# One transfer per weight load, wider loads of x, and a different deal of sums, transposes, taps and scalings in a fused convolution and GELU kernel

## The chip, the cores and the metric

The kernel runs on one core of a Trainium2 chip. A core has five instruction queues that run side by side and meet only through semaphores: TensorE (PE; its weight loads are shown as PEld), VectorE (DVE), ScalarE (ACT), GpSimd (POOL) and SyncE (SP), which here issues only transfers. Each queue is worked through in order. The transfers themselves run on 16 DMA engines that all queues share. Sums and copies run over 128 partitions at once. Results of TensorE go to PSUM, all other operands lie in SBUF. The metric is device time of one execution in microseconds.

## What is computed

The reference, cut to what matters. x is 8 sequences of 4096 tokens with 192 values; 8 heads of 24 values share a 7-tap causal filter each, softmaxed; then a feed-forward block with 2048 hidden values.

```python
w = np.exp(weight - weight.max(-1, keepdims=True))
w = w / (w.sum(-1, keepdims=True) + 1e-09)              # (8 heads, 7 taps)
x_pad = np.concatenate([zeros((B, 6, D)), x], axis=1)
x = einsum('hk,bskhg->bshg', w, windows_of_7(x_pad))    # causal convolution
h = x.reshape(32768, 192) @ w_in                        # w_in: 192 x 2048
g = h * (1.0 / (1.0 + np.exp(-1.702 * h)))              # quick GELU
out = g @ w_out                                         # w_out: 2048 x 192
```

w_in and w_out arrive as float64 and are turned into float32 on the chip, word by word.

## The kernel before

**Tiling.** The work is cut into 32 steps (`N_BIG`). A step takes 512 tokens (`TOK`) of two sequences, kept as two halves o = 0, 1 of 256 tokens on partitions 0-63 and 64-127. Per step the 2048 hidden values are 16 *units* (`NF`) of 128. Every step has two products.

**Hidden product** (`hidden`, L209 matmuls). A unit is three passes of six matmuls into a PSUM slot (a pair of banks, four slots in turn): x and w are split into a high and a low part in a rounded format (fp32r), so that xh with wh (`upper_high`), xl with a low part of w (`upper_low`), then a scaling of the slot by `UP` on ScalarE or VectorE (`scale`, L232), then xd with a third form of w (`lower`), then two GELUs from PSUM into g on ScalarE (`gelu`, L236). On TensorE the order is, for unit i: high part of i, last pass of i-2, low part of i. So a scaling has to be done between the low pass of its unit and the last pass two units on. The string for each unit in `SCALES` deals the two halves' scalings: "a" to ScalarE, "v" to VectorE. wh and half of the low parts stay in SBUF. The other three forms for two units come round through a `ring` of 7 slots, reloaded from `w_dram` by SP as soon as TensorE is done with a slot (`load_ring`, `later`), 24 loads a step.

**Second product** (`second`, L542 matmuls). It follows a list written out by hand (`PLAN`): fast-multiplication sums of blocks of g and of w_out ("spots", each 128 x 1024) replace some products. Ten of the sums of blocks are due while the hidden product still runs (`EARLY_G`); the loop at the end (`extra`) hands them out by unit. Numbers 0 to 4 and 6 to 9 are sums of two spots (L605), number 5 is an accumulating transfer issued from GpSimd (L610): spot 8 takes up spot 0. Sum 3 makes spot 0, sums 6 to 9 need spot 8 after the transfer. Near the end of the second product the next step's first passes are issued ("next").

**x.** Step b+2's x is loaded during step b's hidden product into the last block row of g (`load_x`, `xin_of`), 32 x 32 blocks are transposed on VectorE into `xt` (`transpose_x`, L143, three a step), and taps of the convolution run on ScalarE in the second product (`tap`, L498): each product of a tap goes to a home of its own, and homes are added into `own` by accumulating transfers and by GpSimd (`add_taps`, L515). The last three taps run in the next hidden product, and a tap that reuses a home has to wait for the sum that read it.

**First step** (`first_step`). Weights come in as float64 words, are joined and rounded (`split`, `join`, `rounded`), w_in by pieces of 256 columns: half on partitions 0-63 and half on 64-127, so that after rounding four SP transfers copy them to both halves; then `split_w_in` makes the three forms and stores the streamed ones to `w_dram`. The step's own hidden product waits for each piece. Its second product is plain (`second_plain`), while w_out's forms are made (`add_forms`) by copies on ScalarE and accumulating transfers from GpSimd.

Of the kernel before, what the change touches and what calls it, by code (L numbers as in the profile page):

```python
# [16 lines left out]
def kernel(  # L17
# [27 lines left out]
    XW = NC * Q  # L45
# [73 lines left out]
    x_p = x_v.rearrange("h p s (c v e) -> h p v s c e", c=NC, e=Q)  # L119
# [5 lines left out]
    def load_x(big, part=None):  # L125

        p, c = divmod(big, CHUNKS)
        xin = xin_of(big)
        if c == 0 and not part:
            (nc.gpsimd if big else vec).memset(xin[0:R, :, 0, :], 0.0)  # L130
        for i in range(8) if part is None else (part,):
            n, o, v = i // 4, i // 2 % 2, i % 2
            j = 1 if c == 0 and o == 0 else 0
            t = c * TOK + o * T + (j - 1) * Q
            q0 = o * R + v * Q
            for k in range(NC):
                nc.sync.dma_start(
                    out=xin[q0 : q0 + Q, n, j:NJ, k * Q : (k + 1) * Q],
                    in_=x_p[n, p, v, t : t + (NJ - j) * Q, k, :].rearrange("(j i) e -> i j e", i=Q),
                )  # L140

    def transpose_x(big, c):
        vec.transpose(  # L143
            xt[:, c, :, :].rearrange("p n (j t) -> p (n j) t", t=Q),
            xin_of(big).rearrange("p n j d -> p (n j) d")[:, :, c * Q : (c + 1) * Q],
        )
# [38 lines left out]
    w_dram = dram.tile([STREAM, R, NC * P], F32)  # L185
# [43 lines left out]

    def scale(slot, engines):  # L230
        for o in range(2):
            (act.mul if engines[o] == "a" else vec.tensor_scalar_mul)(slot[o], slot[o], UP)  # L232
# [13 lines left out]
    def hidden(big, tiles, scales, extra, begun=True):  # L246

        for i in range(NF):
            if i or not begun:
                upper_high(tiles[i % 4], i)  # L250
            if i > 1:
                end_unit(big, tiles, i - 2)
            if i or not begun:
                upper_low(tiles[i % 4], i, big)
# [52 lines left out]
    PART = NC * P  # L307
    PIECE = CW * D
    raw = [flat_g(2)[:, 2 * PART * i : 2 * PART * (i + 1)] for i in range(5)]
    raw += [osbs[:, 2 * PART * i : 2 * PART * (i + 1)] for i in range(2)]  # L310
    raw += [flat_own[:, 2 * T : 2 * T + 2 * PART]]
    raw_out = [flat_room[:, 2 * PIECE * i : 2 * PIECE * (i + 1)] for i in range(3)] + [osbs[:, 0 : 2 * PIECE]]
    assert 10 * PART <= 4 * BLK and 2 * PART <= 4 * T and NX <= 4 * BLK and 6 * PIECE <= 5 * BLK
    words_in = [flat_form[:, 2 * PART * i : 2 * PART * (i + 1)] for i in range(2)]
    both_in = [flat_form[:, 2 * PART * i : 2 * PART * (i + 1)] for i in range(2, 4)]
    words_out = [flat_form[:, 8 * PART + 2 * PIECE * i : 8 * PART + 2 * PIECE * (i + 1)] for i in range(2)]
    assert 8 * PART + 4 * PIECE <= FORMS * NG * HD
# [17 lines left out]
    w_in_v = moe_w_in.bitcast(U32).rearrange("(k q) (j h f) -> j h q k f", q=R, j=N_W, h=2)  # L335
# [43 lines left out]
    def in_part(j):  # L379
        return raw[j], words_in[j % 2]  # L380

    def out_piece(i):
        return raw_out[i], words_out[i % 2]
# [32 lines left out]
    def round_w_in(j):  # L416
# [3 lines left out]
        w = m.bitcast(F32)  # L420
        rounded(piece, [(lambda a: a, w)])
# [5 lines left out]
    def split_w_in(j):  # L427
        both = both_in[j % 2]
        act.mul(wh[:, 2 * j : 2 * j + 2].rearrange("p r k f -> p (r k f)"), both, DOWN)  # L429
        nc.gpsimd.tensor_sub(both, both, wide(wh[:, 2 * j : 2 * j + 2].rearrange("p r k f -> p (r k f)")))  # L430
        lows = [t.rearrange("p k f -> p (k f)") for t in (wl[:, j], in_ring(place("l", 2 * j + 1)))]
        for h in range(2):
            act.mul(lows[h], both[:, h * PART : (h + 1) * PART], C)  # L433
        for h in range(2):
            r = 2 * j + h
            to = in_ring(place("d", r)).rearrange("p k f -> p (k f)")
            nc.gpsimd.tensor_sub(to, wide(lows[h]), wide(wh[:, r].rearrange("p k f -> p (k f)")))
        for q in range(3 * j, 3 * j + 3):
            nc.sync.dma_start(out=w_dram[q], in_=wide(in_ring(q))[0:R].rearrange("p k f -> p (k f)"))
# [104 lines left out]
    def second_plain(bx, bs, by, at):  # L544

        mains, sides = (bs[0], bx[0], by[0]), (bx[1], bs[1], by[1])
        rows = [(r, i) for r in (0, 2, 1, 3) for i in range(NG)]
# [56 lines left out]
    def add_up(v, dst, a, op, b):  # L604
        (vec.tensor_add if op == "+" else vec.tensor_sub)(v(dst), v(a), v(b))  # L605

    def sum_g(dst, a, op, b=None):
# [3 lines left out]
        else:  # L611
            add_up(spot, dst, a, op, b)
# [86 lines left out]
    def first_src(c):  # L699
        src = own_of(0) if c == 0 else pairs[1][c - 1].rearrange("p (n t) -> p n t", n=2)  # L700
        return src, 2 * c, 2 * c + 2

    def first_step(tiles):
# [13 lines left out]
        for c in (1, 0, 2):  # L717
            split_high(*first_src(c))
            split_low(*first_src(c))
            split_both(*first_src(c))  # L720
        split_w_in(0)
        load_x(1)
        for i in range(3):
            load_w_out(i)

        def extra(i):
            if i % 2 == 0 and i // 2 + 1 < N_W:
                j = i // 2 + 1
                round_w_in(j)
                if j + 1 < N_W:  # L730
                    split(in_part(j + 1))
                split_w_in(j)
            if i in (9, 10, 11):
                transpose_x(1, i - 9)
            if i == 13:
                split(out_piece(0))
                load_w_out(3)
            if i == 15:
                split(out_piece(1))
                round_w_out(0)  # L740

        hidden(0, tiles, ["av", "vv"] * (NF // 2), extra, begun=False)
        end_unit(0, tiles, NF - 1)
        pf, pa, pb, pc = tiles[3], tiles[1], tiles[0], tiles[2]

        round_w_out(1)
        split(out_piece(2))
        split(out_piece(3))
        round_w_out(2)
        round_w_out(3)  # L750
        load_x(2)
# [3 lines left out]
        def at(i):  # L755
            if i == 0:
# [8 lines left out]
                for c in range(NC):  # L765
                    transpose_x(2, c)
            if i == 2:
# [17 lines left out]
        for c in range(NC):  # L785
            conv(c, 0, times=act.mul)
            for k in range(1, K):
                conv(c, k)
# [69 lines left out]
```

## Time and profile before

| | |
|---|---|
| Median of 3 runs | 2664.82 us (2663.09 to 2668.2) |
| Profiled execution | 2664.49 us, its span 2662.8 us |
| TensorE busy | 2345.8 us, 88% |
| VectorE busy | 1799.4 us, 68% |
| ScalarE busy | 1601.5 us, 60% |
| GpSimd busy | 754.4 us, 28% |
| DMA from GpSimd's queue / SP's queue | 34.3% / 31.7% of 16 engines' span |
| Mean granted TensorE clock | 0.965 |

How to read it: a row of a group has line, engine, operation, tiles written and read, shape, count, then busy time, mean nanoseconds of one, and how long the engine idled before them and for whom. A row of the order of time has start, duration and, in brackets, the idle time before it. A row of the table by stretch has the stretch, then the busy time of TensorE, its weight loads, VectorE, ScalarE and GpSimd with counts, the granted clock, the share of the DMA engines, and GB/s. A row of waits has who waited for whom, the total, how often, and the longest. A row of transfers has count, size and the median time from issue to landing. Matmuls are shown with modelled ends that overlap their followers.

### The profile page before, as it was taken

How to read it: one execution, taken by the hardware profiler on the slowest of the kernel's cores; microseconds unless marked ns; L12 is line 12 of the kernel's file. 1: busy time of each engine (PE TensorE's matmuls, PEld its weight loads, DVE VectorE, ACT ScalarE, POOL GpSimd, SP SyncE). 2: the span in 40 equal slices, each digit the busy share in tenths (PEclk: the TensorE clock that was granted, in tenths of full speed). 3: DMA queues.
4: the chain of work that ended last, by engine and by line, in shares of the span. 5: the costliest groups of instructions: out<-in, count | busy, mean ns of one | idle time of the engine just before them, and what ended most of it. 6: DMA issues, size and time to landing. Idle time of an engine off the chain costs nothing. (4 is left out here: it accounts for less than half of the span.)

```text
span 2662.8 us, 72405 instructions
## 1 busy us (share of the span) xinstructions
PE 2345.8 (88%) x28994; PEld 1561.1 (59%) x28994; DVE 1799.4 (68%) x2536; ACT 1601.5 (60%) x3142; POOL 754.4 (28%) x742
## 2 busy tenths in 40 slices
PE   4576999888999988899988899988999988889898
PEld 2434666556666555566656566656666656566566
DVE  3357667766667766667766667766667766666776
ACT  2444666665666665666665666665666666666654
POOL 1320333132233222233222233222233222233310
PEclk6798999999999999999999999999999999999999
DMA  5264777766777766677766677766667776677754
GB/s 130 58 119 107 151 145 154 155 148 140 148 144 154 158 146 141 147 144 153 153 145 142 147 144 153 154 150 138 146 143 154 155 153 143 144 146 150 159 122 104
DMA packets 525935, 378.64 MB, mean 142 GB/s; under 512 B 365472, under 2 KB 472096, under 8 KB 525600
## 3 DMA queue, kind: packets, MB, share of 16 engines
q0 software_dynamic: 63216, 162.49, 34.3%
q1 hardware_dynamic: 460736, 211.12, 31.7%
q8 instruction: 231, 3.78, 0.6%
q14 instruction: 104, 0.85, 0.1%
q10 hardware_dynamic: 1648, 0.39, 0.1%
HBM read 180.68 MB, written 27.53 MB: 78 GB/s over the span
## 5 line engine op out<-in xcount | busy, mean ns | idle before, releaser
L542 PE MATMUL slot<-g,w_form 128*32 128x256 f32 x8928 | 906.3, 380 | 0.0
L236 ACT ACTIVATE g<-slot 128x512 f32<-128x512 f32 x1024 | 551.0, 594 | 394.6 <-PE slot L209 386.6
L232 DVE TENSOR_SCALAR slot<-slot 128x512 f32<-128x512 f32 x644 | 435.1, 694 | 438.1 <-PE slot L209 404.9
L209 PE MATMUL slot<-xd,ring 64*128 64x512 f32 x3072 | 573.1, 411 | 129.2 <-DVE slot L232 104.6
L209 PE MATMUL slot<-xh,wh 64*128 64x512 f32 x3072 | 541.5, 408 | 91.8 <-ACT wh L429 53.7
L542 PEld LDWEIGHTS slot<-g,w_form 128*32 128x32 f32 x8928 | 476.2, 110 | 143.5 <-issue 11.3
L542 PE MATMUL slot<-g,w_out_s 128*32 128x256 f32 (+1 forms) x6336 | 512.3, 394 | 18.3 <-DVE g L605 14.2
L605 DVE TENSOR_TENSOR g<-g 128x1024 f32<-128x1024 f32 x403 | 484.6, 1215 | 38.1 <-ACT g L236 29.0
L209 PEld LDWEIGHTS slot<-xd,ring 64*128 64x128 f32 x3072 | 355.9, 191 | 252.7 <-DVE slot L232 156.3
L209 PEld LDWEIGHTS slot<-xh,wh 64*128 64x128 f32 x3072 | 359.1, 193 | 186.1 <-ACT g L236 60.1
L653 ACT COPY room<-slot 32x256 f32<-32x256 f32 x651 | 237.7, 365 | 301.3 <-PE slot L542 295.0
L542 PEld LDWEIGHTS slot<-g,w_out_s 128*32 128x32 f32 x6336 | 254.4, 110 | 231.8 <-issue 37.7
L498 ACT ACTIVATE g<-xt,cw 128x512 f32<-128x512 f32 x406 | 286.9, 720 | 108.0 <-POOL own L515 98.9
L209 PE MATMUL slot<-xl,ring 64*128 64x512 f32 x1536 | 280.0, 409 | 60.7 <-DMA ring<-w_dram 59.7
L232 ACT ACTIVATE slot<-slot 128x512 f32<-128x512 f32 x380 | 228.6, 602 | 123.6 <-PE slot L209 123.4
L209 PE MATMUL slot<-xl,wl 64*128 64x512 f32 x1536 | 262.9, 402 | 1.5 <-ACT wl L433 1.5
L610 POOL DMA_DIRECT2D g<-g x124 | 120.1, 969 | 484.3 <-PE slot L542 463.0
L209 PEld LDWEIGHTS slot<-xl,ring 64*128 64x128 f32 x1536 | 174.1, 189 | 123.7 <-DMA ring<-w_dram 98.7
L515 POOL TENSOR_TENSOR own<-own,g 128x512 f32<-128x512 f32 x174 | 229.5, 1340 | 4.6
L542 PE MATMUL slot<-osbs,w_form 128*32 128x256 f32 x2232 | 225.3, 379 | 0.0
L610 POOL DMA_DIRECT2D g<-osbs x31 | 27.1, 874 | 679.3 <-DVE osbs L605 421.4
L143 DVE STREAM_TRANSPOSE xt<-g 128x576 f32<-128x576 f32 x93 | 71.2, 767 | 213.4 <-DMA g<-in_x_dram 213.4
(105 smaller groups left out, 2284.0 us busy)
## 6 DMA issues: line engine op xcount, KB each, us to landing
ring<-w_dram SPq DMA_DIRECT2D x1488, 96.0 KB, 2.4
g<-g POOLq DMA_DIRECT2D x124, 512.0 KB, 7.8
g<-in_x_dram SPq DMA_DIRECT2D x696, 36.0 KB, 2.0
out_dram<-osbs SPq DMA_DIRECT2D x186, 128.0 KB, 2.4
g<-osbs POOLq DMA_DIRECT2D x31, 512.0 KB, 5.4
g<-room POOLq DMA_DIRECT2D x31, 512.0 KB, 5.1
g<-room POOLq DMA_DIRECT2D x58, 256.0 KB, 5.9
g<-g POOLq DMA_DIRECT2D x58, 256.0 KB, 6.9
```

The lines of the kernel that those rows point to most:

```text
L143: vec.transpose(xt[:, c, :, :].rearrange("p n (j t) -> p (n j) t", t=Q), xin_of(big).rearrange("p n j d -> p (n j) d")[:, :, c * Q : (c + ...
L209: nc.tensor.matmul(slot[o], w[halves[o], k, :], t[halves[o], 2 * k : 2 * k + 2, :], start=first and k == KS[0], stop=last and k == KS[-1], ...
L232: (act.mul if engines[o] == "a" else vec.tensor_scalar_mul)(slot[o], slot[o], UP)
L236: act.activation(g[:, r // NG, :, o, r % NG, :], slot[o].rearrange("p (n t) -> p n t", n=2), AF.Gelu_apprx_sigmoid,)
L498: act.mul(home, conv_src(c, k), tap_of(c, k))
L515: eng.tensor_add(dst, dst, home)
L542: nc.tensor.matmul(dst, w, t, start=first, stop=last, skip_group_check=True)
L605: (vec.tensor_add if op == "+" else vec.tensor_sub)(v(dst), v(a), v(b))
L610: nc.gpsimd.dma_start(out=spot(dst), in_=spot(a), accum_op=ALU.add)
L653: act.copy(to, d)
```

## The change

Seven edits:

1. A ring slot is loaded by one transfer of 128 partitions, not by two of 64. `w_dram` holds both halves.
2. x comes in 8 transfers a step with 160 adjoining values (640 bytes) a token, where 24 brought 32 values (128 bytes) each. All 8 are issued in unit 0. The spare columns are not used.
3. The transposes move from units 9, 10, 11 to 5, 6, 7.
4. The last three taps stand in units 0, 2, 4 (were 0, 2, 3), and the sums of homes are in another order.
5. Three of the early sums (numbers 2, 4 and 8) go from VectorE to GpSimd. Sum 0 starts in unit 9. Sums 2 and 4 and the transfer (5) are all given out in unit 11, in that order, on GpSimd's queue.
6. The scalings are dealt anew.
7. The first step's hidden product uses plain float32 matmuls on the rounded w_in itself (`plain`), six a unit, without scaling and without the three passes. w_in is loaded twice, to both halves, so the copies on SP go. The forms of w_in are still made for the later steps, with the two low parts on VectorE instead of ScalarE. w_out's pieces are taken in the order 1, 2, 3, 0, and the convolution for step 2 stands ahead of the turns of the output.

```diff
-    XW = NC * Q
+    XW = D - Q
@@ load_x
-        for i in range(8) if part is None else (part,):
-            n, o, v = i // 4, i // 2 % 2, i % 2
...
-            for k in range(NC):
-                nc.sync.dma_start(
-                    out=xin[q0 : q0 + Q, n, j:NJ, k * Q : (k + 1) * Q],
-                    in_=x_p[n, p, v, t : t + (NJ - j) * Q, k, :].rearrange("(j i) e -> i j e", i=Q),
-                )
+        for n in range(2):
+            for o in range(2):
...
+                for v in range(2):
+                    q0 = o * R + v * Q
+                    nc.sync.dma_start(
+                        out=xin[q0 : q0 + Q, n, j:NJ, :],
+                        in_=x_v[n, p, t : t + (NJ - j) * Q, v * Q : v * Q + XW].rearrange("(j i) d -> i j d", i=Q),
+                    )
@@ load_ring
-            for o in range(2):
-                nc.sync.dma_start(
-                    out=wide(in_ring(q))[halves[o]].rearrange("p k f -> p (k f)"), in_=w_dram[q % STREAM]
-                )
+            nc.sync.dma_start(
+                out=wide(in_ring(q)).rearrange("p k f -> p (k f)"), in_=w_dram[q % STREAM]
+            )
@@
+    def plain(slot, w):
+        for k in KS:
+            for o in range(2):
+                nc.tensor.matmul(
+                    slot[o], w[halves[o], k, :], own[halves[o], 2 * k : 2 * k + 2, :],
+                    start=k == KS[0], stop=k == KS[-1], skip_group_check=True,
+                )
@@ load_w_in
-        for h in range(2):
+        for o in range(2):
             nc.sync.dma_start(
-                out=raw[j][halves[h], :].bitcast(U32).rearrange("p (k f) -> p k f", k=NC), in_=w_in_v[j, h]
+                out=raw[j][halves[o], :].bitcast(U32).rearrange("p (k f) -> p k f", k=NC), in_=w_in_v[j]
             )
@@ round_w_in, split_w_in
-        both = both_in[j % 2]
-        for h in range(2):
-            for o in range(2):
-                nc.sync.dma_start(out=both[halves[o], h * PART : (h + 1) * PART], in_=w[halves[h], :])
...
+    def split_w_in(j):
+        act.mul(wh[:, 2 * j : 2 * j + 2], w_of(j), DOWN)
+        nc.gpsimd.tensor_sub(w_of(j, "rest"), w_of(j), wide(wh[:, 2 * j : 2 * j + 2]))
+
+    def split_rest(j):
+        lows = wl[:, j], in_ring(place("l", 2 * j + 1))
         for h in range(2):
-            act.mul(lows[h], both[:, h * PART : (h + 1) * PART], C)
+            vec.tensor_scalar_mul(lows[h], w_of(j, "rest")[:, h], C)
         for h in range(2):
...
+            nc.gpsimd.tensor_sub(in_ring(place("d", r)), wide(lows[h]), wide(wh[:, r]))
@@ first_step
-        hidden(0, tiles, ["av", "vv"] * (NF // 2), extra, begun=False)
-        end_unit(0, tiles, NF - 1)
+        for i in range(NF):
+            slot = tiles[i % 4]
+            j = i // 2
+            plain(slot, w_of(j)[:, i % 2])
+            if i % 2 == 0:
+                if j + 1 < N_W:
+                    round_w_in(j + 1)
+                split_w_in(j)
+                if j + 2 < N_W:
+                    split(in_part(j + 2))
...
+            else:
+                split_rest(j)
...
+            gelu(slot, i)
@@ first_step, at(0)
                 for c in range(NC):
                     transpose_x(2, c)
+                for c in range(NC):
+                    conv(c, 0, times=act.mul)
+                for c in range(NC):
+                    for k in range(1, K):
+                        conv(c, k)
@@ the steps
-    SCALES = ["av", "vv", "av", "vv", "vv", "av", "vv"] + ["av"] * 9
+    SCALES = ["av"] + ["vv"] * 6 + ["av", "av"] + ["av", "aa", "av", "aa", "av", "av", "aa"]
@@ extra
-            if i < 8 and big + 2 < N_BIG:
-                load_x(big + 2, i)
             if i == 0:
+                if big + 2 < N_BIG:
+                    load_x(big + 2)
                 next_tap()
-                add_taps("c2 4", "c2 1", "fin 0", "fin 1")
-            if i == 1:
                 add_taps("c2 3", eng=vec)
-                add_taps("fin 2")
+                add_taps("c2 4", "c2 1", "fin 0")
             if i == 2:
                 next_tap()
-            if i == 3:
-                add_taps("c2 2", "fin 3")
+                add_taps("c2 2", "c2 5", "fin 1")
+            if i == 4:
                 next_tap()
-            if i == 4:
-                add_taps("c2 5", "c2 6")
+                add_taps("c2 6", "fin 2", "fin 3")
-            if i in (9, 10, 11) and big + 2 < N_BIG:
-                transpose_x(big + 2, i - 9)
-            for j in {10: (0, 3), 11: (4, 1), 12: (5, 2), 13: (6,), 14: (7, 8), 15: (9,)}.get(i, ()):
+            if i in (5, 6, 7) and big + 2 < N_BIG:
+                transpose_x(big + 2, i - 5)
+            for j in {9: (0,), 10: (1, 3), 11: (2, 4, 5), 12: (6,), 13: (7,), 14: (8,), 15: (9,)}.get(i, ()):
                 for item in EARLY_G[j]:
-                    sum_g(*item)
+                    sum_g(*item, eng=nc.gpsimd if j in (2, 4, 8) else vec)
```

More of the change, by code (lines that the diff above doesn't have):

```diff
@@ L184 @@
     STREAM = 3 * N_W
-    w_dram = dram.tile([STREAM, R, NC * P], F32)
+    w_dram = dram.tile([STREAM, P, NC * P], F32)
     def place(what, r):
@@ L244, in end_unit, with hidden @@
         gelu(tiles[r % 4], r)
-    def hidden(big, tiles, scales, extra, begun=True):
+    def hidden(big, tiles, scales, extra):
         for i in range(NF):
-            if i or not begun:
+            if i:
                 upper_high(tiles[i % 4], i)
@@ L252, in hidden @@
                 end_unit(big, tiles, i - 2)
-            if i or not begun:
+            if i:
                 upper_low(tiles[i % 4], i, big)
@@ L306 @@
     CW = NF // NW
-    PART = NC * P
+    PART = 2 * NC * P
     PIECE = CW * D
[L309 to L317, printed above, removed]
+    assert PART == PIECE and NX <= 4 * BLK and 6 * PIECE <= 5 * BLK
+    at_room, at_osbs = ([t[:, 2 * PART * i : 2 * PART * (i + 1)] for i in range(n)] for t, n in ((flat_room, 3), (osbs, 1)))
+    raw = [flat_g(r)[:, 2 * PART * i : 2 * PART * (i + 1)] for r in range(3) for i in range(2)]
+    raw += at_osbs + at_room[0:1]
+    raw_out = at_room + at_osbs
+    sets = [flat_form[:, 2 * PART * i : 2 * PART * (i + 1)] for i in range(4)]
+    words_in, words_out = sets[0:3], (sets[3], sets[0])
+    assert 8 * PART <= FORMS * NG * HD
     diag = flat_room[:, 2 * PIECE : 2 * PIECE + 2 * K * P].rearrange("p (c k q) -> p c k q", c=2, k=K)
```

87 lines of the change are left out of this document (35 added, 52 removed).

## The prediction

> **What bounds the kernel now.** I read the tile view of xl first: it marks every step once. Then the table by stretch of time, for a step with x to load and for the last, which has none; a step is a stretch in which the hidden product runs and one in which the second does.
>
> ```profile
> L170 DVE TENSOR_TENSOR xl<-own,xh x30: 1749/1751/1754, 259.7 to 2557.5; 128x1536 fp32r<-128x1536 f32 x30
> ...
> 1641.30:1690.70 49.40, 42.22 (x360) 30.17 (x359) 28.84 (x39) 27.80 (x52) 12.56 (x10) 0.97 0.56 135
> 1690.70:1721.00 30.30, 30.30 (x560) 18.12 (x560) 26.34 (x39) 22.17 (x47) 11.25 (x13) 1.00 0.92 171
> 2588.00:2627.10 39.10, 37.51 (x358) 29.03 (x354) 26.31 (x35) 24.50 (x48) 0.86 (x1) 1.00 0.47 120
> 2627.10:2657.60 30.50, 30.41 (x560) 18.16 (x560) 23.24 (x38) 10.29 (x29) 4.36 (x5) 1.00 0.50 95
> ```
>
> Steps 1 to 30 are 29 periods in 2297.8 us; with 69.6 (39.1 + 30.5) for the last of them, which loads no x, the other 28 take 79.6 each. The second product takes 30.3 to 30.5 with or without x. The hidden product takes 49.4 against 39.1, so about 10 us a step hang on x and taps, and TensorE sets the rest. Next, the waits, the group by the ring, and SP's and VectorE's order of time in that long stretch:
>
> ```profile
> DVE xt L143 <- DMA g<-in_x_dram: 213.4, 30, 8.5
> ACT g L498 <- POOL own L515: 98.9, 29, 3.4
> ...
> L209 PE MATMUL slot<-xl,ring 64*128 64x512 f32 x1536 | 280.0, 409 | 60.7 <-DMA ring<-w_dram 59.7
> ...
> 1640.83 3.74 SPq L539 DMA_DIRECT2D out_dram<-osbs  x6
> ...
> 1670.09 1.57 SPq L137 DMA_DIRECT2D g<-in_x_dram  x3
> ...
> 1672.41 0.78 DVE L143 STREAM_TRANSPOSE xt<-g 128x576 f32<-128x576 f32 x1 [7.08 <-DMA g<-in_x_dram]
> ```
>
> SP begins x after the stores (1644.6) and issues the last three pieces at 1670.1, since 24 x pieces and three halves a unit of ring loads share its queue. VectorE stands 7.1 us in unit 9's transpose, and the scaling behind it starves TensorE. That, late ring loads, and ScalarE's tap that waits 3.4 us for GpSimd are the 10 us.
>
> **The change, part by part.** *Ring and x loads.*
>
> ```profile
> ring<-w_dram SPq DMA_DIRECT2D x1488, 96.0 KB, 2.4
> g<-in_x_dram SPq DMA_DIRECT2D x696, 36.0 KB, 2.0
> g<-osbs POOLq DMA_DIRECT2D x31, 512.0 KB, 5.4
> g<-g POOLq DMA_DIRECT2D x124, 512.0 KB, 7.8
> ...
> 0.82 11.78 SPq L137 DMA_DIRECT2D g<-in_x_dram  x24
> ```
>
> An x issue costs 0.49 us (11.78/24). Per step SP issues 24 ring loads instead of 48 and 8 x loads instead of 24. The eight go out together in unit 0, after the stores: 3.7 + 3.9 us into the stretch, landed (2.0 to 2.4 more, a price from narrower loads) by about 10. Queued behind them are the first ring loads; seven slots of lead, over four units, hide 4 us. I cost this at nothing; without the cover it is a rival.
>
> *Transposes, taps, scalings.* The three transposes (0.78) move from units 9-11 to 5-7, where x has landed: unit 9's scaling starts 19.5 us into the undisturbed stretch (below) and the pitch is 2.04, so unit 5's starts at 11.3. VectorE has at most two scalings and a transpose there, 1.3 + 0.78 = 2.1 a unit, with over a unit's slack. The last tap moves from unit 3 to 4 and its releasing sum from GpSimd's sixth place to its fourth, so ScalarE's 3.4 us wait goes. So far a step would cost the undisturbed 69.6.
>
> *Three sums on GpSimd.* Here I see the new bound. The accumulating transfer (sum 5, 512 KB) was issued right after VectorE's sum 3. Now it stands on GpSimd's in-order queue behind sums 2 and 4, and VectorE's sum 6, which needs it, stands ahead of the scalings of units 13 and 14. The chain in the undisturbed last step, with prices for GpSimd's sums and for two engines that meet:
>
> ```profile
> 2607.45 0.70 DVE L232 TENSOR_SCALAR slot<-slot 128x512 f32<-128x512 f32 x1 [1.34 <-PE slot L209]
> 2609.49 0.70 DVE L232 TENSOR_SCALAR slot<-slot 128x512 f32<-128x512 f32 x1 [1.34 <-PE slot L209]
> 2610.10 1.22 DVE L605 TENSOR_TENSOR g<-g 128x1024 f32<-128x1024 f32 x1
> 2611.35 1.23 DVE L605 TENSOR_TENSOR osbs<-g 128x1024 f32<-128x1024 f32 x1
> ...
> 2619.04 1.22 DVE L605 TENSOR_TENSOR g<-g 128x1024 f32<-128x1024 f32 x1 [1.25 <-DMA g<-osbs]
> 2620.18 0.69 DVE L232 TENSOR_SCALAR slot<-slot 128x512 f32<-128x512 f32 x1
> ...
> 2618.07 1.06 PE L209 MATMUL slot<-xd,ring 64*128 64x512 f32 x6
> ...
> 2620.93 0.96 PE L209 MATMUL slot<-xd,ring 64*128 64x512 f32 x5 [1.11 <-DVE slot L232]
> ...
> L515 POOL TENSOR_TENSOR own<-own,g x174: 1260/1288/1646, 294.6 to 2530.5; 128x512 f32<-128x512 f32 x174
> ...
> L430 POOL TENSOR_TENSOR w_form<-w_form,wh 128x768 f32<-128x768 f32 x8 | 14.6, 1825 | 94.5 <-ACT wh L429 94.5
> ...
> 121.85 1.01 POOL L437 TENSOR_TENSOR ring<-ring,wh 128x384 fp32r<-128x384 f32 x1
> 122.57 0.71 DVE L396 SCALAR_TENSOR_TENSOR w_form<-own,w_form 128x384 f32<-128x384 uint32 x1
> ...
> 111.37 0.55 DVE L396 SCALAR_TENSOR_TENSOR w_form<-osbs,w_form 128x384 f32<-128x384 uint32 x1
> ...
> 71.73 1.65 PE L209 MATMUL slot<-xh,wh 64*128 64x512 f32 x6 [4.33 <-ACT wh L429]
> ...
> 74.46 1.48 PE L209 MATMUL slot<-xl,wl 64*128 64x512 f32 x6
> ```
>
> Before, sum 3 ends at 2612.58 and sum 6 starts 6.46 later. After: unit 9's scaling ends at 2608.15, sums 0, 1, 3 follow and end at 2611.7. A GpSimd sum of 1024 columns: from 384 to 768 columns it grows by 0.82 us (1.01 to 1.825), so 2.37 (highest: twice the longest 512-column row, 3.3). Do the engines hold each other up? VectorE's two-input operation took 0.71 instead of 0.55 when it began inside GpSimd's, and ended 0.42 after it; GpSimd's longest sum is 0.36 over its median. I take it that they do (lower bound: not at all). So sum 2 starts after sum 3, two sums end at 2616.4, the transfer lands 6.46 later (between 5.4 and 7.8 + 0.5) at 2622.9, sum 6 takes 1.2, and unit 13's scaling ends at 2624.8. The pass that needs it ran at 2618.07: 6.7 us late. Sum 8 then holds GpSimd to 2626.5, VectorE's sum 7 behind it to 2627.7, unit 14's scaling to 2628.4, where that pass ran at 2620.93. TensorE's cold passes after a gap (2.73 for the two from 71.73 to 74.46, at 0.68 each when warm) fit under that wait. A step ends 7.4 late: 77.0 in place of 79.6, **2.6 saved in each of 28 steps, 73 us**; step 31 loses 7.4 and step 30 about 6 (it has a tap wait to lose; an estimate). Step 1 I leave at nothing: its x wait and this wait cancel.
>
> The row of 122.57 is all the trace has on the two engines meeting. [...]
>
> *First step.*
>
> ```profile
> 14.64 14.16 PE L694 MATMUL slot<-xt,room 128*128 128x512 f32 x28 [8.88 <-DVE xt L143]
> ...
> 140.89 5.70 PE L542 MATMUL slot<-g,w_out_s 128*32 128x512 f32 x32 [2.38 <-ACT g L236]
> ...
> 216.51 1.65 PE L209 MATMUL slot<-xd,ring 64*128 64x512 f32 x5 [11.91 <-DVE slot L232]
> ...
> 138.33 0.95 DVE L396 SCALAR_TENSOR_TENSOR w_form<-room,w_form 128x768 f32<-128x768 uint32 x1
> 137.40 0.55 DVE L388 TENSOR_SCALAR w_form<-room 128x768 uint32<-128x768 uint32 x1
> ...
> 166.72 2.56 ACT L296 COPY w_form<-w_out_s 128x384 f32<-128x384 f32 x6
> ...
> 170.20 2.09 DVE L143 STREAM_TRANSPOSE xt<-room 128x576 f32<-128x576 f32 x3
> ...
> 200.59 0.58 ACT L560 COPY room<-slot 32x512 f32<-32x512 f32 x1
> 201.20 1.95 ACT L160 ACTIVATE own<-xt,cw 128x512 f32<-128x512 f32 x3
> ```
>
> x is on its way after 3.9 us of issuing instead of 11.8, so the convolution on TensorE (14.2) begins near 8.5 and the product near 23. Each pair of units then needs, on VectorE, three two-input operations (0.95 each), two one-input (0.55) and two halves (0.35 each, scaled from 0.55): 4.65; on GpSimd 1.825 + 2 x 1.01 = 3.8; on TensorE twelve float32 matmuls of at most 1.0 (14.16 for 14, part of it cold), two abreast if the row halves run together: 6.1. Held apart wholly, the two engines need 8.45, and only for two inputs 6.65; I take 7.6: 61 us for eight pairs, to 84. If the halves do not run abreast it is up to 12 a pair, 35 us more. The second product then starts near 87 instead of 140.9: **54 us**. At its end VectorE's second convolution (13.9 us, the cause of the 11.91) moves ahead of the turns, but three of ScalarE's multiplications move ahead of its form copies, so these start near 173.3 (after 170.20 + 2.09, and the last multiplication) instead of 166.7, and ScalarE's last copy ends near 207.8 instead of 201.2. The pass at 216.51 comes 7 earlier: **7 us**.
>
> Sum, against the profiled execution's 2664.5 (its span 2662.8 and 1.7 around it; the runs' median is 0.3 higher): 2664.5 - 73 + 13 - 61 = **2544 us**.
>
> **The rivals.** *The late transfer is not on the path*, if GpSimd's sums hardly delay it or VectorE reaches sum 6 with work to spare: steps fall to 69.6, and 2664.5 - 61 - 28 x 10 = 2324. For it: the last step shows that nothing else is in the way. Against: the order on both queues. *The burst of x on SP makes ring loads late*: 2 us a step in units 4-6, 56 in all, 2600. For it: ring waits exist today with three x pieces ahead of them; against: SP issues 40 transfers fewer a step. *Slower*: the same chain, longer. With 28 steps at P, two at P against 69.6 and 71, and 61 from the first step, it decides at P = 81.0, 4.0 over my chain. GpSimd's sums at 3.3 (1.9 for two) and the transfer at 8.3 (1.9), with sum 8 in front of sum 7 another 0.9, give P = 81.7, or 2685. For it: 7.8 is the median of its sister transfers; against: 5.4 is its own.
>
> **How the numbers follow.** The forecast has 0.56 and its own range is 2480 to 2610; the burst 0.17; the late transfer off the path 0.13, spread from 2324 to 2450, since part of the wait may stay; longer chain 0.14, of which 0.02 falls within 0.2% (about 5 us, what a measurement here can tell from no change). So faster 0.86, same 0.02, slower 0.12. The range, 2390 to 2660, takes in the half-removed wait below and the chain's bounds up to no gain.
>
> **What would show it.** Right: in late steps VectorE idle about 10 us before one L605 sum, ended by g<-osbs; GpSimd's two 1024-column sums of 2.4 (or longer, if blocked) just ahead of that transfer's issue; hidden stretches of 46 to 47 us; no wait of xt on in_x, hardly any on the ring. Wrong: hidden stretches near 39, waits on ring loads in units 4-7, GpSimd's sums much over 2.4, or a second product of the first step that starts after 100.

## The result and the profile after

The changed kernel takes **2620.5 us** (median of 4 runs, 2613.6 to 2623.0) where the kernel before takes 2664.0 (2661.7 to 2668.2): a ratio of 0.9831, with a 95% interval of 0.9808 to 0.9854. It is 43 us faster. 2544 was forecast, 121 us faster, nearly three times the gain; the range of 2390 to 2660 holds the result. The profiled execution took 2613.6 us, its span 2611.9.

First the first step, TensorE's order of time in the changed kernel: the start of the plain product, of the second product, and of step 1 after its last long wait.

```profile
24.92 7.57 PE L231 MATMUL slot<-own,w_form 64*128 64x512 f32 x34
...
85.85 1.48 PE L547 MATMUL slot<-g,w_out_s 128*32 128x512 f32 x4 [6.90 <-ACT g L242]
...
150.84 1.52 PE L207 MATMUL slot<-xd,ring 64*128 64x512 f32 x3 [17.29 <-ACT slot L238]
```

The second product starts at 85.85 (before: 140.89, forecast "near 87"), and step 1 is under way at 150.84 instead of 216.51: 65.7 us are saved here, 61 were forecast. So all the rest of the program became 15 us *longer* in the two profiled executions: 2613.6 - 150.8 = 2462.8 against 2664.5 - 216.5 = 2448.0.

The steps, by xl in the tile view (one per step), by the table by stretch of one late step of the changed kernel, and by its waits:

```profile
L169 DVE TENSOR_TENSOR xl<-own,xh x31: 1749/1751/1758, 112.1 to 2500.6; 128x1536 fp32r<-128x1536 f32 x31
```
```profile
1664.37:1713.20 48.83, 41.27 (x364) 33.44 (x364) 27.05 (x35) 28.70 (x54) 20.12 (x13) 0.90 0.61 155
1713.20:1744.00 30.80, 30.80 (x566) 18.57 (x560) 26.68 (x41) 22.17 (x47) 11.28 (x13) 1.00 0.88 158
```
```profile
DVE g L610 <- DMA g<-osbs: 292.0, 31, 10.6
...
PE slot L207 <- DVE slot L238: 181.3, 62, 6.4
...
PE slot L207 <- DMA ring<-w_dram: 44.7, 28, 3.4
...
ACT g L503 <- POOL own L520: 8.5, 29, 0.3
...
DVE xt L142 <- DMA g<-in_x_dram: 7.4, 5, 3.0
```

The hidden product still takes 48.8 us where 39.1 would do (49.4 before), at a granted clock of 0.90. The waits of before are gone: VectorE for x (213.4 us before; 7.4 now, and 12.1 that the view puts down to the ring, though a transpose reads only x), ScalarE's tap for GpSimd (98.9, now 8.5). A new one has their place: VectorE for the transfer g<-osbs, 292.0 us, 9.4 a time, and behind it TensorE for VectorE's scalings. This is the chain that the prediction laid out. In the order of time of that step:

```profile
1687.20 2.36 DVE L610 TENSOR_TENSOR osbs<-g 128x1024 f32<-128x1024 f32 x2
...
1688.56 3.27 POOL L610 TENSOR_TENSOR osbs<-osbs,g 128x1024 f32<-128x1024 f32 x1 [9.49 <-DVE osbs L610]
...
1689.48 0.69 DVE L238 TENSOR_SCALAR slot<-slot 128x512 f32<-128x512 f32 x1
...
1691.78 2.41 POOL L610 TENSOR_TENSOR room<-g,osbs 128x1024 f32<-128x1024 f32 x1
...
1694.12 0.85 POOL L615 DMA_DIRECT2D g<-osbs  x1
...
1699.51 1.23 DVE L610 TENSOR_TENSOR g<-g 128x1024 f32<-128x1024 f32 x1 [9.34 <-DMA g<-osbs]
1700.66 0.69 DVE L238 TENSOR_SCALAR slot<-slot 128x512 f32<-128x512 f32 x1
1700.88 2.35 POOL L610 TENSOR_TENSOR g<-g 128x1024 f32<-128x1024 f32 x1 [5.91 <-DVE g L610]
1701.26 3.07 DVE L610 TENSOR_TENSOR room<-g 128x1024 f32<-128x1024 f32 x1
1701.40 1.64 PE L207 MATMUL slot<-xd,ring 64*128 64x512 f32 x5 [5.12 <-DVE slot L238]
...
1704.25 0.69 DVE L238 TENSOR_SCALAR slot<-slot 128x512 f32<-128x512 f32 x1
...
1704.98 1.65 PE L207 MATMUL slot<-xd,ring 64*128 64x512 f32 x5 [0.65 <-DVE slot L238]
...
1711.62 1.23 DVE L610 TENSOR_TENSOR g<-g 128x1024 f32<-128x1024 f32 x1 [5.57 <-ACT g L242]
```

Sums 1 and 3 on VectorE, then sums 2 and 4 on GpSimd, the transfer behind them, sum 6 waiting 9.34 us for it, unit 13's scaling, and TensorE 5.12 us idle ahead of its pass. Sum 8 on GpSimd then holds VectorE's sum 7 (3.07 us instead of 1.22) ahead of unit 14's scaling. In this step unit 13's pass starts 37.0 us after the start of the stretch and unit 14's 40.6; the prediction had 36.8 and 40.4. But the five matmuls of those passes take 1.64 and 1.65 us, and from unit 14's scaling to the last row, the first sum of the second product, which waits for the last GELU, there are 7.4 us. Behind the gap TensorE works at half its clock: a pass of six matmuls takes 0.68 us ahead of it and 1.28 behind it (1702.43 to 1703.71), and the clock granted from 1701.95 to 1705.36 is 0.50.

To compare kernels I cut every step at four rows: xl, VectorE's first scaling of the next hidden product, GpSimd's issue of the transfer, sum 6. Mean us of 28 steps, read from the order of time of each profile. The forecast's row is worked out of the prediction's numbers: issue at 28.4, sum 6 at 34.9, end at 46.5 after the start of the stretch, the first scaling 1.7 after it.

| kernel | xl to first scaling | to the issue | to sum 6 | to next xl | step | time, one profiled run |
|---|---|---|---|---|---|---|
| before | 32.2 | 33.9 | 13.4 for both | | 79.5 | 2664.5 |
| forecast | 32.2 | 26.7 | 6.5 | 11.6 | 77.0 | 2544 |
| after | 32.2 | 28.5 | 5.5 | 13.2 | 79.5 | 2613.6 |
| 3: transfer first | 32.2 | 24.8 | 5.7 | 12.5 | 75.2 | 2479.8 |
| 1: and sum 6 later | 32.2 | 24.9 | 5.6 | 9.4 | 72.2 | 2390.9 |
| 2: sums on VectorE | 32.2 | 24.0 | 5.9 | 9.1 | 71.2 | 2354.5 |
| 4: sum 8 on VectorE | 32.2 | 29.1 | 5.5 | 11.4 | 78.2 | 2572.9 |
| 7: before, with edit 5 | 32.2 | 38.9 | 5.5 | 12.8 | 89.5 | 2968.5 |
| 5: first gap filled | 32.2 | 29.0 | 5.6 | 12.1 | 78.9 | 2595.3 |
| 10: both gaps filled | 32.2 | 28.9 | 5.6 | 11.6 | 78.3 | 2576.9 |
| 11: and x spread | 32.2 | 27.0 | 5.5 | 11.6 | 76.3 | 2520.4 |
| 6: as 2, x spread | 32.2 | 26.3 | 5.8 | 9.0 | 73.3 | 2418.9 |
| 9: as 2, x in unit 2 | 32.2 | 23.1 | 5.9 | 8.4 | 69.6 | 2312.1 |
| 8: as 6, transposes later | 32.2 | 22.7 | 5.9 | 8.4 | 69.2 | 2299.2 |

Kernels 1 to 11 ran once each, in sessions in which the kernel before took from 2664.5 to 2674.1 us, so a difference of less than about 10 us between rows of different sessions shows nothing by itself.

### The profile page after: what moved, and what is told of

It reads as the page before. It is cut to its first block, busy times and chain, and to the rows that moved or that the text cites. A ratio compares the mean times of both kernels' runs of the same rounds, so it can differ in the third digit from the quotient of the medians.

```text
span 2611.9 us, 69454 instructions
## 1 busy us (share of the span) xinstructions
PE 2323.7 (89%) x28898; PEld 1626.8 (62%) x28898; DVE 1749.5 (67%) x2398; ACT 1607.9 (62%) x3148; POOL 997.5 (38%) x835
## 4 chain that ended last, share of the span: by engine, by line
PE 56%; DMA 14%; DVE 11%; POOL 8%; SPq 5%; issue 4%; ACT 2%; DVEq 0%; POOLq 0%; ACTq 0%
PE slot L547 40%; PE slot L207 17%; DMA ring<-w_dram 6%; DMA g<-osbs 6%; DVE room L610 4%; POOL osbs L610 4%; SPq L136 3%; POOL room L610 3%; DVE g L610 3%; ACT g L242 1%; SPq L544 1%; DVE osbs L610 1%; DVE slot L238 1%; DVE osbs L534 1%; DMA room<-in_moe_w_in_dram 1%
## 5 line engine op out<-in xcount | busy, mean ns | idle before, releaser
L547 PE MATMUL slot<-g,w_form 128*32 128x256 f32 x8928 | 940.1, 384 | 0.0
L610 DVE TENSOR_TENSOR g<-g 128x1024 f32<-128x1024 f32 x372 | 447.5, 1216 | 463.9 <-DMA g<-osbs 292.0
L207 PE MATMUL slot<-xd,ring 64*128 64x512 f32 x2976 | 516.6, 425 | 243.3 <-DVE slot L238 181.3
L547 PEld LDWEIGHTS slot<-g,w_form 128*32 128x32 f32 x8928 | 485.1, 111 | 144.1 <-issue 11.4
L547 PE MATMUL slot<-g,w_out_s 128*32 128x256 f32 (+1 forms) x6336 | 546.0, 414 | 24.4 <-DVE g L610 17.5
L238 DVE TENSOR_SCALAR slot<-slot 128x512 f32<-128x512 f32 x589 | 392.0, 695 | 203.8 <-PE slot L207 199.5
L207 PE MATMUL slot<-xh,wh 64*128 64x512 f32 x2976 | 434.7, 390 | 0.0
L207 PEld LDWEIGHTS slot<-xh,wh 64*128 64x128 f32 x2976 | 305.2, 185 | 45.3 <-issue 13.2
L610 POOL TENSOR_TENSOR osbs<-osbs,g 128x1024 f32<-128x1024 f32 x31 | 100.8, 3251 | 353.6 <-DVE osbs L610 208.1
L207 PE MATMUL slot<-xl,wl 64*128 64x512 f32 x1488 | 217.6, 390 | 0.0
L547 PE MATMUL slot<-room,w_form 128*32 128x256 f32 x2232 | 171.5, 379 | 0.0
```

Source lines behind the costliest of these rows:

```text
L207: nc.tensor.matmul(slot[o], w[halves[o], k, :], t[halves[o], 2 * k : 2 * k + 2, :], start=first and k == KS[0], stop=last and k == KS[-1], ...
L547: nc.tensor.matmul(dst, w, t, start=first, stop=last, skip_group_check=True)
L610: (eng.tensor_add if op == "+" else eng.tensor_sub)(v(dst), v(a), v(b))
```

## The experiments

### What costs the ten microseconds: the order on GpSimd's queue

The theory: of the whole change, edit 5 alone makes the new wait. Four kernels take it apart. Kernel 1 moves the transfer to the front of GpSimd's queue and sum 6 behind unit 13's scaling.

```diff
-            for j in {9: (0,), 10: (1, 3), 11: (2, 4, 5), 12: (6,), 13: (7,), 14: (8,), 15: (9,)}.get(i, ()):
+            for j in {9: (0,), 10: (1, 3), 11: (5, 2, 4), 13: (6, 7), 14: (8,), 15: (9,)}.get(i, ()):
```

> Sums 2, 4 and 8 stay on GpSimd; transfer 5 is given out ahead of sums 2 and 4, and sum 6 moves behind the scaling of unit 13, where it was before. Queue order is the cause (theory): sum 3 ends 25.2 after the start of the stretch (1689.56 - 1664.37 in the changed kernel), the transfer lands about 6.5 later, at 31.7, while unit 13 is already scaled; the 5.1 us gap and the cold passes behind it go, a step falls from 79.4 to 70 to 72, and the time to 2340 to 2390. The burst of x and ring loads on SP is the cause (rival): nothing moves, 2580 to 2615. [...]

Kernel 2 gives all sums back to VectorE.

```diff
-            for j in {9: (0,), 10: (1, 3), 11: (2, 4, 5), 12: (6,), 13: (7,), 14: (8,), 15: (9,)}.get(i, ()):
+            for j in {10: (0, 3), 11: (4, 1), 12: (5, 2), 13: (6,), 14: (7, 8), 15: (9,)}.get(i, ()):
...
-                    sum_g(*item, eng=nc.gpsimd if j in (2, 4, 8) else vec)
+                    sum_g(*item, eng=vec)
```

> Edit 5 undone: all ten sums on VectorE in the units they had before, the rest of the change kept. Queue order behind GpSimd's sums is the cause (theory): the rest of the change is worth about 10 us a step as forecast, a step takes 70 to 72, the time is 2340 to 2390. The burst on SP, the moved transposes or the redealt scalings cost the time (rival): steps stay above 76, 2520 to 2615. VectorE cannot hold 3.7 us more of sums in units 10 to 14 (second rival): steps of 73 to 75, 2430 to 2490.

Kernel 3 changes the order on the queue and nothing else: `11: (5, 2, 4)` in place of `11: (2, 4, 5)`.

> Only the order on GpSimd's queue: transfer 5 ahead of sums 2 and 4, sum 6 still ahead of the scalings of units 13 and 14. The transfer is then issued 3.6 us earlier (two sums of GpSimd less ahead of it, less the 2.4 that overlap with sum 3 and VectorE). Theory with the clock: TensorE's gap falls from 5.1 to about 1.6 us, too short to make it cold, and 3.5 + 2 us a step go: steps of 74, 2430 to 2480. Theory without the clock: 3.5 us a step go, steps of 76, 2500 to 2530. Rival that the order does not matter: 2600 to 2615.

Measured: 2390.9, 2354.5 and 2479.8 us. Kernel 2 is where the theory put it, kernel 1 just above its upper edge, kernel 3 at 75.2 a step between the two theories of it, its time at the upper end of the one with the clock. That a gap of 1.6 us is too short to make TensorE cold was an estimate: in the kernel before, between the first 250 and the last 100 us, 106 gaps of 1.0 to 1.9 us began at a clock of 1.00, and within 3.5 us behind 12 of them the clock fell to 0.50; in kernel 5 (below) it fell behind the one of 1.95 us in 10 of 28 steps. Moving one DMA issue ahead of two sums is worth 134 us. The burst of x and the redealt scalings are not the main cause: kernel 2 keeps them. In its waits VectorE stands 20.9 us for the transfer instead of 292.0, and what is left on TensorE is the ring:

```profile
PE slot L207 <- DMA ring<-w_dram: 48.3, 27, 3.0
...
DVE g L610 <- DMA g<-osbs: 20.9, 28, 2.3
```

Kernel 7 does the opposite: the kernel before with edit 5 alone (its deal and `eng=nc.gpsimd if j in (2, 4, 8) else vec`).

> The kernel before with edit 5 alone: sums 2, 4 and 8 on GpSimd and the sums in their new units; x, ring, transposes, taps, scalings and the first step as they were. Theory (GpSimd's two sums put the transfer 3.7 us later and the chain behind it is on the path, on top of the late x): a step grows from 79.6 to about 88, the time to 2860 to 2920. Rival (the wait for x and the wait for the transfer overlap, as the prediction assumed for step 1): 2650 to 2720. Rival that edit 5 is a gain by itself, since VectorE has less to do: below 2650.

Measured 2968.5 us, 304 slower than before and above the theory's 2860 to 2920; a step takes 89.5 (about 88 was expected). The issue of the transfer moves from 33.9 to 38.9 after the first scaling, 5.0 where 3.7 was expected, and the wait for it adds to the wait for x:

```profile
DVE g L605 <- DMA g<-osbs: 253.1, 31, 8.7
DVE xt L143 <- DMA g<-in_x_dram: 213.0, 30, 8.5
```

The wait for x is as long as before (213.4) and the new one stands behind it. So the two do not cancel. Edit 5 costs 304 us on the kernel before and 259 on the changed one (2613.6 - 2354.5), where the other edits together gain 310 (2664.5 - 2354.5).

### Sum 8 and its hold on sum 7

Kernel 4 gives only sum 8 back to VectorE: `j in (2, 4)`.

> The changed kernel with only sum 8 back on VectorE; sums 2 and 4 stay on GpSimd ahead of the transfer. Theory (sum 8 holds VectorE's sum 7 by 3.07 - 1.22 = 1.85 us, and sum 7 stands ahead of unit 14's scaling): the stretch from sum 6 to the next split of x falls from 13.2 by up to 1.9 us, the first part of a step is unchanged, the time is 2555 to 2575. [...] Second rival (sum 8's 1.2 us on VectorE give half of it back): 2575 to 2600.

Measured 2572.9. Every sum of that shape now takes 1.22 us (in the changed kernel every other one took 3.07):

```profile
L610 DVE TENSOR_TENSOR room<-g x62: 1214/1220/1226, 185.1 to 2536.3; 128x1024 f32<-128x1024 f32 x62
```

From sum 6 to the next xl it is 11.4 instead of 13.2: the hold of 1.85 us lay on the path as a whole. Sum 8's own 1.2 us on VectorE come behind the scaling and cost nothing in that column. A step falls by less, 79.5 to 78.2, since the issue of the transfer comes 0.6 later; why is open.

### Is TensorE's clock the missing term?

Kernel 5 leaves the chain alone and fills TensorE's gap ahead of unit 13's last pass with matmuls whose results are overwritten.

```diff
+            if i == NF - 1:
+                for _ in range(20):
+                    for o in range(2):
+                        nc.tensor.matmul(
+                            tiles[0][o], wh[halves[o], 0, 0, :], xh[halves[o], 0:2, :],
+                            start=True, stop=True, skip_group_check=True,
+                        )
```

> The changed kernel with 20 pairs of matmuls (both row halves, 128x512 of input each pair) whose results are overwritten, put on TensorE between the first pass of unit 15 and the last pass of unit 13, where TensorE stands 5.1 us; at 0.227 a pair they take 4.5 us, so the chain of sums is untouched and only the gap is filled. The cold clock is the missing term (theory): the passes behind the gap run at 0.68 instead of 1.3, a step loses about 2 us, 77.4, and the time is 2545 to 2575. The clock costs nothing there, since the next wait takes it up (rival): 2605 to 2620. The added matmuls come too late themselves or are slower than priced (second rival): above 2620.

Measured 2595.3, between the theory and its rival. The table by stretch, from unit 14's scaling to the end of the last GELU, tells why. Two steps of the changed kernel (the second number is the length, the third from the end the granted clock):

```profile
1704.25:1711.59 7.34, 6.69 (x69) 3.36 (x71) 1.80 (x3) 4.73 (x8) 0.00 (x0) 0.69 0.28 77
1862.38:1867.97 5.59, 4.94 (x69) 2.67 (x71) 1.81 (x3) 4.73 (x8) 0.00 (x0) 1.00 0.35 104
```

And two of kernel 5:

```profile
1686.56:1692.14 5.58, 4.84 (x67) 2.67 (x71) 1.80 (x3) 3.91 (x6) 0.00 (x0) 1.00 0.26 74
1842.73:1849.93 7.20, 6.46 (x67) 3.11 (x71) 1.81 (x3) 3.91 (x6) 0.00 (x0) 0.76 0.21 58
```

The stretch takes 5.6 at a clock of 1.00, and 7.1 to 8.4 at 0.60 to 0.76. In the changed kernel 24 of 28 steps are of the long kind (mean of all 7.32), in kernel 5 ten (mean 6.16). All 28 steps of kernel 5 have a second gap, of 1.9 to 2.2 us, ahead of unit 14's pass, and in those ten the clock falls to 0.50 behind it. Kernel 10 fills that as well, with 8 pairs.

```diff
+        for _ in range(8):
+            for o in range(2):
+                nc.tensor.matmul(
+                    tiles[0][o], wh[halves[o], 0, 0, :], xh[halves[o], 0:2, :],
+                    start=True, stop=True, skip_group_check=True,
+                )
         end_unit(big, tiles, NF - 2)
```

> The changed kernel with the gap of 5.1 us filled as before, and with 8 more pairs of overwritten matmuls in the second gap, 1.95 us ahead of unit 14's last pass. With the first gap alone filled, 18 of 28 steps took 5.6 us from unit 14's scaling to the last activation at a granted clock of 1.00, and 10 took 7.2 at 0.76. Theory (the clock is the whole of that difference): all 28 take 5.6, the mean falls from 6.16 to 5.6, and the time by 16 us to 2575 to 2585. Rival (something else held these ten): 2590 to 2600, and the stretch stays at 7.2 in some steps at a clock of 1.00.

Measured 2576.9, as the theory had it: 27 of 28 steps take 5.6 and one 6.8, at 0.89. So the clock is the whole of that difference: 13.2 becomes 11.6 in the last column, the forecast's own number.

### Is the ring late because of x?

In its steps' hidden products kernel 2 has hardly another wait on TensorE than the 48.3 us for the ring. Kernel 6 is kernel 2 with x given out two loads a unit.

```diff
-    def load_x(big):
+    def load_x(big, part=None):
...
+                if part not in (None, 2 * n + o):
+                    continue
...
+            if i < 4 and big + 2 < N_BIG:
+                load_x(big + 2, i)
```

> The kernel with all sums on VectorE, and in addition the eight loads of x given out two a unit in units 0 to 3 instead of all in unit 0. The burst makes ring loads late (theory; TensorE waits 48.3 us for the ring in that kernel, 28 times, about 1.7 us a step): the ring waits fall below 15 us and the time from 2354.5 to 2300 to 2325. Rival (a ring load that runs beside x lands late however x is given out): ring waits stay above 35 us, 2345 to 2360. Second rival (x now lands too late for the transpose of unit 5): a wait of xt on x of 1 us a step or more, above 2360.

Measured 2418.9, slower than kernel 2: the second rival. TensorE's wait for the ring fell to 14.2 us, but VectorE now stood in unit 5's transpose, which this view puts down mostly to the ring:

```profile
DVE xt L144 <- DMA ring<-w_dram: 127.2, 26, 7.0
...
DVE xt L144 <- DMA g<-in_x_dram: 15.6, 4, 4.5
PE slot L209 <- DMA ring<-w_dram: 14.2, 15, 2.8
```

A transpose reads only x, so it is x that was late: the ring's loads stand between x's parts on the same queue. In the order of time SP's issues stand as the program gives them out (in the changed kernel's step above the stores from 1663.89, x from 1667.82, the ring loads from 1671.88), and a ring load there waits for its slot to come free (836.1 us in 566 waits for TensorE in the changed kernel). In the step at 1550 us SP issues the last two parts of x from 1559.15 on, and unit 5's transpose begins at 1567.10, after a wait of 3.96 us that the order of time puts down to x. Kernel 8 therefore moves the transposes to units 7 to 9 too (`if i in (7, 8, 9)`).

> All sums on VectorE, x given out two loads a unit in units 0 to 3, and now the transposes in units 7 to 9 instead of 5 to 7. Theory (the ring is late because x goes out in one burst ahead of it, and the spread x was late only for the early transposes): ring waits about 14 us in all as in the spread kernel, no wait of xt, and 1.5 us a step less than with the burst: 2300 to 2325. Rival (x behind ring loads on SP comes so late that VectorE waits in unit 7 too): xt waits over 50 us, 2340 to 2420.

Kernel 9 keeps x in one burst but gives it out in unit 2, so that the first ring loads go ahead of it, with the same late transposes.

> All sums on VectorE, the eight loads of x together as in the changed kernel but given out in unit 2 instead of unit 0, transposes in units 7 to 9. Theory (what makes the ring late is x right behind the stores, which hold SP 4 us already): the first ring loads go out ahead of x, ring waits under 20 us, time 2300 to 2330. Rival (the burst moves the same wait four units on): ring waits above 40 us, 2345 to 2365.

Measured 2299.2 and 2312.1, kernel 9 within its theory's stretch and kernel 8 just under it. In kernel 8's waits the ring and x are small, though not gone (kernel 9 waits 20.9 us for the ring, where its theory had under 20):

```profile
DVE xt L144 <- DMA ring<-w_dram: 21.1, 21, 2.0
...
PE slot L209 <- DMA ring<-w_dram: 10.5, 15, 1.3
```

Both orders take away most of the ring's wait, so it was the eight loads of x right behind the stores, ahead of every ring load, that made the ring late. Kernels 8 and 9 also move the transposes; that alone, with x in one burst in unit 0, was not run, but in kernel 6 the ring's wait falls without it.

### Do the two terms make up the miss?

Kernel 11 is the changed kernel, its chain of sums and transfer as it was, with both gaps filled and x spread (transposes in units 7, 8 and 11).

> The changed kernel, its chain of sums and transfer untouched, with both filled gaps and with x spread over units 0 to 3 (transposes in units 7, 8 and 11, so that no sum of the chain comes later). Theory (the prediction's chain is right, and what it missed are the clock and the ring behind x): about 1.6 us a step less than with both gaps filled, 2525 to 2550, the time that the prediction gave. Rival (the ring's wait is not on the path of this chain, as VectorE and GpSimd make up for it before the transfer): 2565 to 2580. Second rival (VectorE waits for x in unit 7 and the chain starts later): above 2580.

Measured 2520.4, 5 below the expected stretch; a step takes 76.3, where the prediction had 77.0. The two terms account for the miss, and for more: without them the kernel is faster than forecast, since the transfer is 1.0 us a step shorter than priced.

### The best version

Kernel 12 is kernel 8 again, timed.

> The kernel with all sums on VectorE, x spread over units 0 to 3 and transposes in units 7 to 9, timed in rounds. If its one time of 2299.2 stands, the median is 2290 to 2310 and the ratio to the kernel before 0.858 to 0.866; a median above 2320 would say that single time was lucky.

Measured 2297.6 us (5 runs, 2293.6 to 2298.6) against 2669.2 of the kernel before on that chip: a ratio of 0.8606 (0.8594 to 0.8618). Against the changed kernel's median, taken in another session, it is 12% faster. The page of kernel 8's execution has TensorE at

```profile
PE 2206.5 (96%) x28898; PEld 1526.7 (66%) x28898; DVE 1804.7 (79%) x2491; ACT 1606.0 (70%) x3148; POOL 755.2 (33%) x742
```

That is the change with edit 5 undone, the rest kept, and x taken out of the ring's way.

## Why the prediction was right in kind and too high in gain

**The first step** was right: 65.7 us against 61, the second product at 85.85 against 87, (85.85 - 24.92) / 8 = 7.6 us a pair as taken. That mean is partly luck. Pairs that nothing else held did take 7.5 to 7.7 in VectorE's order of time, but the first three took 5.2 each on TensorE, one took 10.2 while GpSimd waited 6.6 for a store to `w_dram`, and the last 6.9 are a wait for ScalarE.

**The chain of edit 5** was right in place and nearly in time (37.0 and 40.6 against 36.8 and 40.4; sum 4 on GpSimd 2.41 against 2.37). Kernels 1, 2, 3 and 7 show that it is what bounds a step, and that the rival "the late transfer is not on the path" was wrong. Its transfer came 1.0 us sooner than priced: 6.46 had been measured from the end of a VectorE sum, which had 0.5 us to the issue, where GpSimd's own sum has none, and in that step it landed in 5.9, where the median now is 5.3. That the times of the passes agree so well is luck in part: in the step shown the issue came 29.8 after the start instead of 28.4, and the shorter transfer made up for most of it.

**Two steps failed.** The first is the sentence "TensorE's cold passes after a gap ... fit under that wait". It looked at the two passes between the scalings of units 13 and 14. They do fit (0.65 us of wait is left), but the clock stays low behind them: the passes and products from unit 14's scaling on took 7.32 us instead of 5.6, 1.7 a step. Kernels 5 and 10 show it. In the changed kernel the clock stood at 0.60 to 0.70 over that stretch in 24 of 28 steps, behind gaps of about 5 us (5.12 in the step shown); in kernel 5 it fell behind gaps of 2.2 us and less as well, in 10 of 28 (last section).

The second is "I cost this at nothing", of x on SP ahead of the ring. The cover, "seven slots of lead, over four units", was not enough. The issues took what was priced: in the step shown the first ring load goes out 7.5 us after the start. The landing did not. A load of x landed in 4.3 us, not in the 2.0 to 2.4 taken from narrower ones, and ring loads right behind x in 5.3 instead of 2.4 (first two rows: medians of the execution; last two: of the loads of that step, issued from 1667.8 to 1676.5),

```profile
ring<-w_dram SPq DMA_DIRECT2D x744, 192.0 KB, 2.4
g<-in_x_dram SPq DMA_DIRECT2D x232, 180.0 KB, 4.3
...
g<-in_x_dram SPq DMA_DIRECT2D x8, 180.0 KB, 4.2
ring<-w_dram SPq DMA_DIRECT2D x7, 192.0 KB, 5.3
```

and TensorE waits 44.7 / 28 = 1.6 us a step for the ring. The loads of x also became larger: 8 x 180 KB a step, with the spare columns, where 24 x 36 KB came before, 1.7 times as much. The rival of the burst had 2 us a step for this, on top of the same chain; it came true, together with the clock's term, which no case had. Kernels 6, 8 and 9 show it, and kernel 11 against 10 is 1.95 us a step.

**The account.** Issue 1.8 later, transfer 1.0 shorter, the tail 1.6 longer: 2.5 us more a step than forecast (79.49 against 77.0), 28 x 2.5 = 70 us. That is 2613.6 - 2544. The rest of the sum cancels. The first step gained 5 more than forecast; step 1 behind it took 3 longer than before, where nothing was forecast; steps 30 and 31 took 6.6 and 6.0 longer, against about 6 and 7.4 in the prediction; and a step of before is 79.5 by the tile view, not 79.6, which makes 2 us in 28. The three other runs took 6 to 9 us more than the profiled one; the cause is open.

**"So far a step would cost the undisturbed 69.6"**, that is, without edit 5: 71.2 in kernel 2, and 69.2 once the ring was freed. That the step has about 10 us to give was right; edit 5 took back 8.3 of them (79.5 against 71.2). And "its x wait and this wait cancel", assumed for step 1, was 3 us off there, and it does not hold as a rule: in kernel 7 the two add.

**Slower** was given 0.12 and would have needed a step of 81.0. The measured 79.5 is 1.5 short of it; without the 65.7 of the first step the change would have lost.

## What to carry to other kernels

A DMA issue stood here behind the sums on its queue (28.5 us after the first scaling, 24.8 with two sums fewer ahead of it, and 134 us less in all): put it ahead of the sums on that engine, and only then ask whether the engine has room for them. When a stall of several microseconds stays in front of TensorE, charge not only the stall but also the matmuls behind it at half clock, beyond the next wait too, for as long as the trace shows it (here, behind gaps of 5 to 6 us, 7.2 to 8.4 us from unit 14's scaling on, where 5.6 would do at a clock of 1.00). A burst on a queue that also feeds a ring has to fit within the ring's lead with the landing time under that load (here 5.3 us for ring loads right behind x, against 2.4); here, spreading it or putting it behind the first ring loads cost nothing once its consumer moved along.

## What the runs showed of the hardware

**GpSimd also held up VectorE's operations with one input.** In the first step of the changed kernel 18 of the 24 one-input operations of this shape (L393, L394) took 0.55 to 0.57 us; the six that began inside a GpSimd sum took 1.11 to 2.17. One of them, which ended after the sum:

```profile
40.21 2.41 POOL L434 TENSOR_TENSOR w_form<-w_form,wh 128x768 f32<-128x768 f32 x1 [1.07 <-ACT wh L433]
40.87 2.17 DVE L393 TENSOR_SCALAR w_form<-g 128x768 uint32<-128x768 uint32 x1
42.96 0.55 DVE L394 TENSOR_SCALAR w_form<-g 128x768 uint32<-128x768 uint32 x1
```

2.17 in place of 0.55. The hold lies in the operation's own time, not in a wait ahead of it, so here these two queues do not meet only through semaphores. The prediction had left open whether it takes in operations with one input: it took 7.6 us a pair, between 6.65 and 8.45. The first step still did not become dearer than forecast: the pairs took the 7.6 us that the prediction had. The scalings from PSUM to PSUM were not held: the 300 that began inside a GpSimd sum took 0.69 to 0.70, as the one at 1689.48 above.

**Short gaps lowered the clock too.** In kernel 5 no wait of TensorE for a scaling on VectorE is longer than 2.2 us, and in 10 of 28 steps the clock fell to 0.50 behind the one of 1.95. In the changed kernel the clock was back at 1.00 by unit 14's scaling in 4 of 28 steps, with gaps of 5.0 to 6.0 before it. So neither its fall nor its return went by the length of the gap alone. Between the first 250 and the last 100 us of the changed kernel each stay of the clock at 0.50 lasted 3.41, 6.83 or 10.24 us, and each at 1.00 between them 6 to 21 times 3.41, so I counted TensorE's busy share in stretches of 3.41 us from one change of the clock to the next. Here are two steps of kernel 5, each with the stretch that holds the second gap and the one behind it (of the engines, TensorE's busy time alone):

```profile
1840.72:1844.13 3.41, 1.48 (x13) 1.00 0.41 115
1844.13:1847.54 3.41, 3.41 (x35) 0.50 0.24 62
...
1683.70:1687.11 3.41, 1.65 (x12) 1.00 0.34 100
1687.11:1690.52 3.41, 3.22 (x41) 1.00 0.29 78
```

The stretch at 1840.72 is busy for 43% and the clock falls behind it; the one at 1683.70 is busy for 48%, and the clock stays. In that part of the changed kernel all 31 falls follow a stretch busy for at most 46%, and every stretch at full clock that is busy for less than 45% is followed by one; the clock returned behind a stretch busy for 83% or more, and stayed low behind one of 81% or less. In these traces the fall thus went with the busy share of such a stretch. The shares come from matmuls with modelled ends, and in the kernel before the line is less sharp (falls follow stretches busy for up to 61%), so they are a finding of these traces and no rule.
